# Attention into two expert layers: row sums from a column of ones, and one transpose for two heads

## The chip, the core and the metric

One core of a Trainium2 chip runs the whole program. Its engines run side by side, each through its own queue in order: PE multiplies matrices (PEld is its weight load), DVE, ACT and POOL work element by element, and SP issues the transfers (DMA). An engine that waits for another holds everything behind the waiting instruction. The metric is the device time of one execution in microseconds; less is better.

## What is computed

```python
B, H, S, D = 4, 8, 576, 64
scores = np.matmul(q, k.transpose(0, 1, 3, 2)) / sqrt(D)
x = (log1p(abs(rel)) / psi_i)[..., None]          # rel[i, j] = i - j
bias = np.maximum(x @ w1 + b1, 0.0) @ w2          # 32 hidden, one bias per head
scores = scores + bias.transpose(2, 0, 1)[None]
attn = exp(scores - max(scores)); attn = attn / (sum(attn) + 1e-09)
x = np.matmul(attn, v)          # -> 2304 tokens x 512
r = np.maximum(x @ w_in, 0.0); x = (s * r * r + b) @ w_out       # 512 -> 2048 -> 512
h = x @ w_in2; out = (h - np.tanh(h)) @ w_out2                   # 512 -> 2048 -> 512
```

In the text the first layer after attention is MoE1 and the second MoE2.

## The kernel before

Every float32 operand of a product is split into two float16 parts, hi and lo, and a product is made of several float16 products (hi x hi, hi x lo, lo x hi). DVE, ACT and POOL do the splitting: a cast gives hi, and a subtraction gives lo.

**Bias.** For each of 36 blocks Q of 16 rows, `hid` (L717, instructions at L727 on ACT and L730 on DVE or POOL) makes the 32 hidden values for up to 576 distances in tiles `hid`, `hr` or `xt_own` (whichever memory is free then), PE multiplies them into `pb` (L761), `out` (L766, through `copy_scale`, L611 on DVE, L615 on ACT) writes the row and its mirror image into a tile `et`, and SP sends it to a buffer `btd` in memory, from which `bi` is read row by row.

**Attention.** 36 groups of four units; a unit is one head on 128 rows of queries (or two heads on 64). For a unit, `qk` (L1030) multiplies queries and keys into `sp` (two units in one go), `ttr` (L1073, DVE) adds the bias and takes the minimum of the negated scores, `mx_add` (L1081) adds a constant to it, `ex` (L1087, ACT) takes the exponential `e` and, by a read of ACT's accumulator, its row sum, `hi` (L1097 DVE, L1099 ACT) and `lo` (L1104) split `e` into `hl`, `tr` (L1119) turns `hl` over by a DMA transpose of nine 128x128 blocks (five of hi, four of lo, the fifth being shared) into `et`, and `pv` (L1132 for v's hi part, L1138 for its lo part) multiplies `et` with the values `vp` into the PSUM tile `xp`, of which there is one buffer for the four units of a group. When a group is done, `x_tasks` adds a small constant to the sums (`eps`, L1176), takes reciprocals (L1180), scales `xp` (L1188), splits the result and turns it over by transposes of four blocks (L1217) for MoE1.

**MoE1** starts while attention runs. For a block of 256 tokens, `ph` (L1573) is the first product, `relu` (L1586) and `square` (L1591) follow on ACT, the result is split into `hr` (`hi` L1597 DVE or L1599 ACT, `lo` L1603), and `po` (L1645) is the second product, whose output leaves PSUM at L1659 (DVE) or L1664 (ACT) as `x`. `norm` (L1554) stands before the first `ph`. **MoE2** starts when attention's memory is free: its weights are converted and prepared there (`w2big`, `w1big`; L618 writes a low part), and then seven block products in place of eight run through `pa`, `pb` (L2038) and `acc` (L2166).

**The order.** Nothing is issued in the order of the program text. `Schedule` holds all tasks with the engines that each may use, an estimated duration for each, what it depends on, which tiles it takes from a ring of buffers and a priority. `forward` plays them through with a clock for each engine, takes the task that can start first, with priorities to decide between tasks that can start at almost the same time, and so writes out each engine's queue. The tables `COST` and `XFER` multiply the estimates of operations and transfers, `ENGINE` limits a task to an engine, `SHIFT` adds to priorities, and `PORT` says which DVE tasks the planner keeps from running beside POOL's. The rings hold two `e`, three `hl`, four `et` and four `bi`; `ENGINE` and these tables name tasks by stage and function (`u3.hi`: cast of the exponentials in the third stretch of units).

## Time and profile before

| | |
|---|---|
| time, median of 3 runs | 1053.97 us (1053.57 to 1055.98) |
| the profiled execution | 1057.96 us |
| its span in the trace | 1056.2 us |
| granted clock of PE over the span, mean | 0.954 |
| busy: PE, DVE, ACT, POOL | 964.1 (91%), 881.6 (83%), 667.5 (63%), 250.1 us (24%) |
| instructions on PE, DVE, ACT, POOL | 13486, 1918, 1307, 319 |
| row sums (L1087, accumulator reads) | 144, 28.1 us on ACT |
| DMA transposes of exponentials (L1119) | 144, from 66.6 to 566.1 us |

The span is the time from the first to the last instruction in the trace, and the time of an execution has a little around it. An engine's share of busy time is an average over stretches with different limits, so that it must be read by stretch. A group of instructions is a line of the program on one engine, with the tiles written and read; "x28 | 13.8, 498" says that 28 instructions took 13.8 us in all, 498 ns each in the mean. What stands behind the second bar is the engine's idle time just before them, with what ended it.

### The profile page before, as it was taken

How to read it: one execution, taken by the hardware profiler on the slowest of the kernel's cores; microseconds unless marked ns; L12 is line 12 of the kernel's file. 1: busy time of each engine (PE TensorE's matmuls, PEld its weight loads, DVE VectorE, ACT ScalarE, POOL GpSimd, SP SyncE). 2: the span in 40 equal slices, each digit the busy share in tenths (PEclk: the TensorE clock that was granted, in tenths of full speed). 3: DMA queues.
4: the chain of work that ended last, by engine and by line, in shares of the span. 5: the costliest groups of instructions: out<-in, count | busy, mean ns of one | idle time of the engine just before them, and what ended most of it. 6: DMA issues, size and time to landing. Idle time of an engine off the chain costs nothing.

```text
span 1056.2 us, 32450 instructions
## 1 busy us (share of the span) xinstructions
PE 964.1 (91%) x13486; PEld 833.2 (79%) x13486; DVE 881.6 (83%) x1918; ACT 667.5 (63%) x1307; POOL 250.1 (24%) x319
## 2 busy tenths in 40 slices
...
GB/s 341 398 227 216 311 236 119 184 200 252 245 197 230 168 179 176 201 188 207 171 180 104 397 21 138 148 36 12 32 23 32 52 23 22 42 22 23 22 22 22
DMA packets 261444, 153.66 MB, mean 145 GB/s; under 512 B 197680, under 2 KB 229552, under 8 KB 261296
## 3 DMA queue, kind: packets, MB, share of 16 engines
...
## 4 chain that ended last, share of the span: by engine, by line
PE 43%; DVE 9%; ACT 3%; DMA 2%; issue 2%; POOL 1%; SPq 0%; DVEq 0%; ACTq 0%; POOLq 0%
PE acc L2166 14%; PE pa L2038 9%; PE pb L2038 7%; PE po L1645 5%; PE ph L1573 4%; PE po L2166 2%; DMA et<-hl 2%; DVE w2big L1852 2%; DVE w2big L618 1%; PE sp L1041 1%; DVE w1big L618 1%; ACT e L1087 1%; POOL hl L1104 1%; PE xp L1132 1%; DVE hr L1603 1%
## 5 line engine op out<-in xcount | busy, mean ns | idle before, releaser
L1645 PE MATMUL po<-hr,w1big 128*128 128x256 f16 x1728 | 202.9, 274 | 3.6 <-ACT x L1664 2.7
L1104 POOL TENSOR_TENSOR hl<-e,hl 128x64 f16<-128x64 f32 (+1 forms) x200 | 160.2, 818 | 184.9 <-ACT hl L1099 107.2
L1573 PEld LDWEIGHTS <-w1big 128*128 128x128 f16 x1728 | 166.9, 99 | 31.5 <-issue 10.6
L1645 PEld LDWEIGHTS <-w1big 128*128 128x128 f16 x1728 | 165.5, 98 | 26.5 <-issue 7.1
L2038 PEld LDWEIGHTS <-w2big 128*128 128x128 f16 x3024 | 175.2, 99 | 2.2 <-issue 2.1
L2166 PEld LDWEIGHTS <-w1big 128*128 128x128 f16 x3024 | 172.8, 98 | 0.0
L1087 ACT ACTIVATE e<-sp,mx 128x576 f32<-128x576 f32 x144 | 105.6, 735 | 70.3 <-POOL mx L1081 34.3
L1073 DVE CUSTOM_DVE_ANT_0 sp<-sp,bi 128x576 f32<-128x576 f32 x144 | 107.0, 772 | 20.2 <-PE sp L1041 16.2
L1573 PE MATMUL ph<-xt_own,w1big 128*128 128x256 f16 x960 | 113.1, 274 | 3.0 <-ACT r L1586 2.2
L1041 PE MATMUL sp<-ks,qs 64*128 64x288 f16 (+1 forms) x960 | 84.2, 296 | 25.8 <-ACT e L1087 24.8
L1573 PE MATMUL ph<-w1big 128*128 128x256 f16 x768 | 91.2, 276 | 3.3 <-ACT r L1586 2.6
L1041 PEld LDWEIGHTS <-qs 64*128 64x128 f16 (+1 forms) x960 | 48.7, 99 | 53.0 <-issue 42.2
L1132 PEld LDWEIGHTS <-et 128*128 128x128 f16 (+1 forms) x1440 | 54.7, 104 | 41.2 <-issue 21.5
L1132 PE MATMUL xp<-vp,et 128*128 128x64 f16 (+1 forms) x1440 | 65.4, 199 | 19.1 <-DMA et<-hl 11.7
L2166 PE MATMUL acc<-hr,w1big 128*128 128x128 f16 x1296 | 79.9, 219 | 0.0
L1099 ACT ACTIVATE hl<-e 128x576 f16<-128x576 f32 x96 | 64.7, 678 | 23.1 <-DMA et<-hl 20.2
L2166 PE MATMUL acc<-w2big,w1big 128*128 128x128 f16 x1296 | 79.0, 219 | 0.0
L1104 DVE TENSOR_TENSOR hl<-e,hl 128x512 f16<-128x512 f32 (+1 forms) x88 | 48.8, 572 | 15.9 <-ACT hl L1099 13.0
L2038 PE MATMUL pa<-w1big,w2big 128*128 128x128 f16 x960 | 59.9, 219 | 1.7 <-ACT w2big L2057 0.9
L1586 ACT ACTIVATE r<-ph 128x512 f32<-128x512 f32 x72 | 42.3, 590 | 25.8 <-PE ph L1573 21.3
L1591 ACT ACTIVATE r<-r,sq 128x512 f32<-128x512 f32 x72 | 51.2, 718 | 0.9
L2074 ACT ACTIVATE w1big<-w1big 128x512 f32<-128x512 f32 x34 | 21.3, 630 | 45.6 <-DVE w1big L2064 33.4
...
## 6 DMA issues: line engine op xcount, KB each, us to landing
...
```

Of the source, the lines that this page charges most:

```text
L1041: nc.tensor.matmul(out=out, lhsT=qs.tile[64 * h:64 * h + 64, sq, p * r:p * r + r], rhs=ks.tile[64 * h:64 * h + 64, sk, half * HS:(half + 1 ...
L1073: nc.vector.tensor_tensor_reduce(out=st, in0=st, in1=bi.tile.rearrange("p (a b) -> p a b", a=2), scale=-1.0 / KAP, scalar=3.0e38, op0=ALU. ...
L1087: nc.scalar.activation(out=put(e, row_tile("e")).rearrange("p (a b) -> p a b", a=2), in_=sp.tile[:, :, 0:HS], func=AF.Exp, scale=-1.0, bia ...
L1099: nc.scalar.activation(out=h[:, 0:S], in_=e.tile, func=AF.Copy)
L1104: eng_of(eng).tensor_tensor(out=hl.tile[:, o:o + m], in0=e.tile[:, c:c + m], in1=hl.tile[:, c:c + m], op=ALU.subtract)
L1132: nc.tensor.matmul(out=xp[r0:r0 + r, o:o + 64], lhsT=et.tile[:, n, r0:r0 + r], rhs=vp.tile[:, 0, n % 5, 64 * h:64 * h + 64], start=n == 0, ...
L1573: nc.tensor.matmul(out=ph.tile[:, fi, :], lhsT=win_ap(1, sw, m, f), rhs=xa(sx, m), start=m == 0 and j == 0, stop=m == KM - 1 and j == 2,)
L1586: nc.scalar.activation(out=r.tile, in_=ph.tile, func=AF.Relu)
L1591: nc.scalar.activation(out=r.tile, in_=r.tile, func=AF.Square, scale=sq[:, fp // 4:fp // 4 + 1])
L1645: nc.tensor.matmul(out=po.tile[:, :NB1], lhsT=wout_ap(1, sw, f, c), rhs=rhl[f // 8][:, f % 8, sr, :], start=f == 0 and j == 0, stop=f == K ...
L2038: nc.tensor.matmul(out=bank.tile[:, f * HT:(f + 1) * HT], lhsT=w[:, sw, m, f * 128:(f + 1) * 128], rhs=xs[:, sx, m], start=p in (1, 2, 5) ...
L2166: nc.tensor.matmul(out=bank.tile[:, o + c * HT:o + (c + 1) * HT], lhsT=w[:, sw, f, c * 128:(c + 1) * 128], rhs=g[:, sx, f], start=new and ...
```

## The change

The changed kernel makes the row sums of the softmax on PE. The hi part of `vp` gets a 65th column of ones for each head (a memset, `ones`), nine of the 14 `pv` matmuls of a unit write 65 columns, and `xp` has 260 columns in place of 256. The exponential no longer reads the accumulator, and the order that the sums imposed on the exponentials of a group is gone; `eps` reads the sums out of `xp` when all four `pv` of the group are done, on DVE alone.

The exponentials of two units share one tile `hl` and one tile `et` of twice the size. One DMA transpose of 18 blocks takes the place of two of nine, and the `pv` of both units come after it. The rings hold two of each, where they held three `hl` and four `et`. Two blocks Q of the bias share an `et` tile as well.

More tasks may choose their engine: `mx_add` may go to ACT (50 of 144 do), `hid` of every block Q to POOL (`QG` from 7 to 36), `relu` to DVE (11 of 72 do), and the copies of the first products out of PSUM to DVE (17 do, at L2057 in the kernel before). The matrix of ones on the diagonal that `norm_max` multiplies with is bfloat16. The planner's estimates, its hops between engines and the tables are new; of the tables one or two lines stand here.

```diff
-SHARE0, QP, QA, SCU, QG = 21, 8, 16, 12, 7
+SHARE0, QP, QA, SCU, QG = 21, 8, 16, 12, 36
...
-AHEAD = 6.97
+AHEAD = 8.21
...
-    "x.recip": 0.0,
+    "x.recip": 0.0, "x.eps": 0.0,
...
-    "s1.lambda": "dve", "f1.hi": "act", "bias3.out": "act", "bias4.lambda": "dve", "k1.hi": "act", "f2.hi":
+    "s1.lambda": "dve", "f1.hi": "act", "bias3.out": "act", "bias4.lambda": "act+dve", "f2.hi": "dve",
...
-    HOP = dict(pe=0.57, act=-0.03, dve=0.16, pool=0.37, turn=0.0)
+    HOP = dict(pe=0.57, act=-0.05, dve=0.12, pool=0.41, turn=0.0)
...
-                    elif eng == "pool" and t.opts[eng] < self.LONG:
+                    elif eng == "pool" and t.share > 0.0 and t.opts[eng] < self.LONG:
...
-    ROWS = dict(bi=4, e=2, hl=3, et=4)
+    ROWS = dict(bi=4, e=2, hl=2, et=2)
...
-    xp_all = ps_x.tile([128, 256], F32, name="xp")
+    xp_all = ps_x.tile([128, 260], F32, name="xp")
...
-        t = row_p.tile([128, S + 16 if name == "et" else S], F32, tag=name, name=name, bufs=ROWS[name])
-        return t if dt == F32 else t[:, :S].bitcast(dt)
+        n = {"et": 2 * S + 32, "hl": 2 * S}.get(name, S)
+        t = row_p.tile([128, n], F32, tag=name, name=name, bufs=ROWS[name])
+        return t if dt == F32 else t[:, :min(n, 2 * S)].bitcast(dt)
...
-    eye32 = const.tile([128, 128], F32, name="eye32")
+    eye16 = const.tile([128, 128], BF16, name="eye16")
...
             if Q < QG:
-                opts[POOL] = 4.2e-3 * n
+                opts[POOL] = 5.0e-3 * n
...
-        ev = inst("et")
+        ev = ev_of[Q] = ev_of[Q - 1] if Q % 2 else inst("et")
+        eo = Q % 2 * (S + 16)
...
-            o = put(ev, row_tile("et"))
+            o = (ev.tile if Q % 2 else put(ev, row_tile("et")))[:, eo:]
...
-        t_ev = [sc.add({ACT: 0.87, DVE: 0.80}, out, t_bmm[Q], d, [ev], [i])]
+        t_ev = [sc.add(
+            {ACT: 0.87, DVE: 0.80}, out, t_bmm[Q] + (t_evs[Q - 1] if Q % 2 else []), d, [] if Q % 2 else [ev], [i, ev]
+        )]
+        t_evs[Q] = t_ev
...
-            t = put(vp, vp_p.tile([128, 2, VW], F16, tag="vp", name="vp").rearrange("p s (n c) -> p s n c", c=128))
-            copy_scale(t[:, 0], src(), sc_t[b]["v"], eng)
+            t = vp_p.tile([128, 2 * VW + 10], F16, tag="vp", name="vp")
+            put(vp, (
+                t[:, :VW + 10].rearrange("p (n h d) -> p n h d", h=2, d=65),
+                t[:, VW + 10:].rearrange("p (n h d) -> p n h d", h=2, d=64),
+            ))
+            copy_scale(vp.tile[0][:, :, :, 0:64], src().rearrange("p n (h d) -> p n h d", h=2), sc_t[b]["v"], eng)
...
+        def ones(eng):
+            eng_of(eng).memset(vp.tile[0][:, :, :, 64:65], 1.0)
+        to = sc.add({POOL: 0.15, DVE: 0.1}, ones, [th], due - 2, [], [vp], share=0.0)
...
-        vp, sm_i, xp_i = vp_t[b, p], sum_of[n], xp_of[n]
+        e = inst("e")
+        odd = k % 2
+        hl, et = hl_of[u], et_of[u] = (hl_of[u - 1], et_of[u - 1]) if odd else (inst("hl"), inst("et"))
+        h0 = odd * 2 * S
+        vp, xp_i = vp_t[b, p], xp_of[n]
         mx = {}
...
-        t_mx = sc.add({DVE: 0.16, POOL: 0.3}, mx_add, [t_ttr[u]], d + 1.5)
+            if eng == ACT:
+                nc.scalar.activation(out=m, in_=m, func=AF.Copy, bias=LN_E)
+            else:
+                eng_of(eng).tensor_scalar(out=m, in0=m, scalar1=LN_E, scalar2=None, op0=ALU.add)
+        t_mx = sc.add({DVE: 0.16, POOL: 0.31, ACT: 0.2}, mx_add, [t_ttr[u]], d + 1.5)
 
...
-            if k == 0:
-                put(sm_i, sm.tile([128, NP], F32, tag="sum", name="sum"))
             nc.scalar.activation(
                 out=put(e, row_tile("e")).rearrange("p (a b) -> p a b", a=2), in_=sp.tile[:, :, 0:HS], func=AF.Exp,
-                scale=-1.0, bias=mx["m"][:, 0:1], accum_out=sm_i.tile[:, col:col + 1],
-            )
-        t_exp[u] = sc.add({ACT: 0.78}, ex, [t_mx], d + 2, [e] + ([sm_i] if k == 0 else []), [sp, sm_i],
-                           [t_exp[u - 1]] if k else [])
+                scale=-1.0, bias=mx["m"][:, 0:1],
+            )
+        t_exp[u] = sc.add({ACT: 0.695}, ex, [t_mx], d + 2, [e], [sp])
...
-            h = put(hl, row_tile("hl", F16))
+            h = (hl.tile if odd else put(hl, row_tile("hl", F16)))[:, h0:h0 + S]
...
+        if not odd:
+            return
+
         def tr(_):
             nc.sync.dma_start_transpose(
                 out=put(et, row_tile("et", F16).rearrange("p (n r) -> p n r", r=128)), in_=hl.tile
             )
-        t_tr[u] = sc.add({SP: (1.25, 1.4)}, tr, t_lo, d + 5 - 500, [et], [hl])
+        t_tr[u] = t_tr[u - 1] = sc.add({SP: (1.4, 2.8)}, tr, t_los[u - 1] + t_lo, d + 5 - 500, [et], [hl])
+        for v in (u - 1, u):
+            unit_pv(v)
+
+    def unit_pv(u):
...
-            o = col * 64
+            o = col * 65
...
-                        out=xp[r0:r0 + r, o:o + 64], lhsT=et.tile[:, n, r0:r0 + r],
-                        rhs=vp.tile[:, 0, n % 5, 64 * h:64 * h + 64], start=n == 0, stop=False,
+                        out=xp[r0:r0 + r, o:o + 65], lhsT=et.tile[:, e0 + n, r0:r0 + r],
+                        rhs=vp.tile[0][:, n % 5, h], start=n == 0, stop=False,
...
-            {PE: 0.42 if full else 0.85}, pv, [t_tr[u], t_vlo[b, p], t_pv.get(u - 1)], d + 10 - 1000,
+            {PE: 0.42 if full else 0.85}, pv, [t_tr[u], t_pv.get(u - 1)] + t_vlo[b, p], tau(u) + 10 - 1000,
...
-        def eps(eng):
-            ri = sum_of[n].tile
-            eng_of(eng).tensor_scalar(out=ri, in0=ri, scalar1=1e-9 * 2.0 ** 15, scalar2=None, op0=ALU.add)
-        te = sc.add({DVE: 0.16, POOL: 0.3}, eps, [t_exp[u] for u in us], d - 3, [], [sum_of[n]])
+        sums = inst("sum")
+        x65 = lambda: xp_of[n].tile.rearrange("p (h d) -> p h d", d=65)
+
+        def eps(_):
+            t = put(sums, sm.tile([128, NP], F32, tag="sum", name="sum"))
+            nc.vector.tensor_scalar(
+                out=t, in0=x65()[:, :, 64], scalar1=1e-9 * 2.0 ** 15, scalar2=None, op0=ALU.add
+            )
+        te = sc.add({DVE: 0.18}, eps, [t_pv[u] for u in us], d - 502, [sums], [xp_of[n]], share=0.0)
 
         def recip(_):
-            nc.vector.reciprocal(out=sum_of[n].tile, in_=sum_of[n].tile)
-        te = sc.add({DVE: 0.17}, recip, [te], d - 2, [], [sum_of[n]])
+            nc.vector.reciprocal(out=sums.tile, in_=sums.tile)
+        te = sc.add({DVE: 0.17}, recip, [te], d - 501, [], [sums])
 
         xf = inst("xf")
 
         def scale(_):
-            x = xp_of[n].tile.rearrange("p (h d) -> p h d", d=64)
+            x = x65()[:, :, 0:64]
             put(xf, x_p.tile([128, 256], F32, tag="xf", name="xf", bufs=2))
             nc.vector.tensor_tensor(
                 out=xf.tile.rearrange("p (h d) -> p h d", d=64), in0=x,
-                in1=sum_of[n].tile.unsqueeze(2).to_broadcast([128, NP, 64]), op=ALU.mult,
-            )
-        t_xs[n] = sc.add({DVE: 0.41}, scale, [t_pv[u] for u in us] + [te], d - 500, [xf], [sum_of[n], xp_of[n]], share=0.0)
+                in1=sums.tile.unsqueeze(2).to_broadcast([128, NP, 64]), op=ALU.mult,
+            )
+        t_xs[n] = sc.add({DVE: 0.41}, scale, [te], d - 500, [xf], [sums, xp_of[n]], share=0.0)
...
-            nc.tensor.matmul(out=pm.tile, lhsT=m.to_broadcast([128, 128]), rhs=eye32, start=True, stop=True)
+            nc.tensor.matmul(out=pm.tile, lhsT=m.to_broadcast([128, 128]), rhs=eye16, start=True, stop=True)
...
+                if e == DVE:
+                    nc.vector.tensor_scalar(out=r.tile, in0=ph.tile, scalar1=0.0, scalar2=None, op0=ALU.max)
+                else:
+                    nc.scalar.activation(out=r.tile, in_=ph.tile, func=AF.Relu)
...
-                {ACT: 0.68}, lambda _: nc.scalar.activation(out=home(i), in_=bank.tile, func=AF.Copy, scale=ich),
-                [t] + (first_use["E"] if k < 2 else []), pr - 300, [i], [bank],
+                {ACT: 0.68, DVE: 0.66}, lambda e: copy_scale(home(i), bank.tile, ich, e),
+                [t] + (first_use["E"] if k < 2 else []), pr - 300, [i], [bank], share=0.0,
```

Because the planner writes the queues, the order of the work moves too, in three places above all.

On DVE, at the start of the program, `u_sb` is the table of logarithms from which the hidden layer is made in `hr`; `gram`, `qk_t`, `qk_y` and `qkc` belong to the scan that gives the scales of queries and keys. Before:

```order
L701 TENSOR_SCALAR u_sb<-w1big,cst_sb 128x576
L730 TENSOR_SCALAR hr<-u_sb,cst_sb 128x576 x2
L730 TENSOR_SCALAR hr<-u_sb,cst_sb 128x560 x2
L730 TENSOR_SCALAR hr<-u_sb,cst_sb 128x544 x2
L896 TENSOR_REDUCE s_0_127<-gram 128x2
L730 TENSOR_SCALAR hr<-u_sb,cst_sb 128x528 x2
L815 TENSOR_SCALAR qk_t<-psum 128x2
L807 TENSOR_SCALAR qk_y<-qk_t 128x2
```

And in the changed kernel, the same place:

```order
L706 TENSOR_SCALAR u_sb<-w1big,cst_sb 128x576
L907 TENSOR_REDUCE s_0_127<-gram 128x2
L826 TENSOR_SCALAR qk_t<-psum 128x2
L818 TENSOR_SCALAR qk_y<-qk_t 128x2
L823 TENSOR_SCALAR qk_t<-qk_y 128x1
L829 SCALAR_TENSOR_TENSOR qk_t<-qk_t,qk_y 128x1
```

The hidden layer has left this place of DVE's queue; ACT and POOL do it.

On SP, where the transposes of the first units meet the bias rows that are written to memory (`btd<-et`) and read back (`bi<-btd`) and the loads of MoE1's weights (`w1big<-in_wout`). Before:

```order
L468 DMA w1big<-in_wout 128x2x1024
L468 DMA bi<-btd_119 128x576 x2
L1119 DMA_TRANSPOSE et<-hl 128x9x128 x3
L468 DMA bi<-btd_119 128x576 x2
L468 DMA btd_121<-et 128x591 x2
L1119 DMA_TRANSPOSE et<-hl 128x9x128
L1217 DMA_TRANSPOSE xt_own<-xh 128x4x128
L1119 DMA_TRANSPOSE et<-hl 128x9x128 x2
```

And in the changed kernel:

```order
L472 DMA w1big<-in_wout 128x2x1024
L1149 DMA_TRANSPOSE et<-hl 128x18x128
L472 DMA btd_120<-et 128x591 x2
L472 DMA bi<-btd_119 128x576 x2
L1149 DMA_TRANSPOSE et<-hl 128x18x128
L472 DMA btd_121<-et 128x591 x2
L1149 DMA_TRANSPOSE et<-hl 128x18x128
```

One issue stands where two stood, and it stands where the second of a pair stood or later: no `pv` of a pair can begin before it.

On PE, at the end of MoE1, each matmul has a weight load before it in the queue. Before, the first product of MoE2 (`pa`, with weights `w2big`) comes straight behind 144 `po`, and only products follow:

```order
L1645 LDWEIGHTS w1big
L1645 MATMUL po<-hr,w1big 128x256
L2038 LDWEIGHTS w2big
L2038 MATMUL pa<-w1big,w2big 128x128
L2038 LDWEIGHTS w2big
```

In the changed kernel 96 `po` stand before the first `pa`, and 48 more come after 24 matmuls each of `pa` and `pb`; this is the place where `pb` ends and those 48 begin:

```order
L2089 LDWEIGHTS w2big
L2089 MATMUL pb_11412<-w1big,w2big 128x128
L1696 LDWEIGHTS w1big
L1696 MATMUL po<-hr,w1big 128x256
L1696 LDWEIGHTS w1big
```

Up to the last `pv`, PE's queue holds 1104 `po` and 1248 `ph` before the change, 1056 and 1248 after it.

## Rows read from the trace of the kernel before

**Rows 1.** Windows: stretch and length us, busy us (count) PE PEld DVE ACT POOL, clock, DMA, GB/s

```profile
20.00:160.00 140.00, 92.70 (x891) 51.07 (x892) 133.66 (x266) 104.69 (x216) 61.35 (x55) 0.73 0.96 281
...
200.00:560.00 360.00, 348.06 (x4641) 289.25 (x4637) 261.43 (x719) 246.24 (x557) 154.96 (x236) 1.00 0.99 198
560.00:620.00 60.00, 54.71 (x574) 47.62 (x573) 39.06 (x78) 29.78 (x72) 1.64 (x3) 0.97 0.65 213
620.00:703.00 83.00, 77.72 (x705) 68.69 (x704) 80.64 (x124) 64.63 (x115) 0.00 (x0) 1.00 0.32 101
703.00:724.00 21.00, 15.34 (x230) 14.79 (x228) 20.20 (x26) 15.35 (x21) 0.00 (x0) 0.90 0.03 9
724.00:1056.00 332.00, 328.19 (x5845) 328.02 (x5843) 300.33 (x605) 163.31 (x246) 0.00 (x0) 0.99 0.09 28
```

**Rows 2.** Waits: engine, line, releaser: us in all, times, longest (PE from 150 us)

```profile
PE sp L1041 <- ACT e L1087: 8.8, 14, 2.3
PE xp L1132 <- DMA et<-hl: 5.6, 6, 2.5
...
ACT hl L1099 <- DMA et<-hl: 20.2, 22, 2.5
```

**Rows 3.** Groups of DVE: line, form, count, busy us, mean ns, idle before

```profile
L618 DVE SCALAR_TENSOR_TENSOR w2big<-w2big,w_c 128x1024 f16<-128x1024 f32 x14 | 17.6, 1280 | 0.4 <-ACT w2big L615 0.4
...
L1659 DVE TENSOR_SCALAR x<-po,esc,bcol 128x128 f32<-128x128 f32 (+1 forms) x41 | 14.4, 395 | 19.7 <-PE po L1645 19.7
L730 DVE TENSOR_SCALAR hid<-u_sb,cst_sb 128x400 f32<-128x400 f32 (+8 forms) x27 | 14.0, 556 | 2.1 <-PE pb L761 2.0
L1597 DVE CAST hr<-r 128x512 f16<-128x512 f32 x28 | 13.8, 498 | 7.7 <-ACT r L1591 7.6
...
L730 DVE TENSOR_SCALAR hr<-u_sb,cst_sb 128x576 f32<-128x576 f32 (+6 forms) x12 | 6.6, 593 | 3.8 <-PE pb L761 3.8
...
L611 DVE TENSOR_SCALAR et<-pb,cst_sb 128x496 f32<-128x496 f32 (+11 forms) x12 | 5.7, 519 | 0.3 <-PE pb L761 0.3
```

**Rows 4.** Groups of ACT, and one of POOL

```profile
L1087 ACT ACTIVATION_READ_ACCUMULATOR e<-sp,mx 128x1 f32 x144 | 28.1, 195 | 0.0
L615 ACT ACTIVATE et<-pb,cst_sb 128x576 f32<-128x576 f32 (+59 forms) x60 | 26.9, 500 | 17.5 <-PE pb L761 16.7 <-DMA btd<-et 0.7
...
L727 ACT ACTIVATE hr<-u_sb,cst_sb 128x416 f32<-128x416 f32 (+14 forms) x36 | 20.9, 644 | 1.2 <-DVE u_sb L701 1.2
...
L730 POOL TENSOR_SCALAR hr<-u_sb,cst_sb 128x512 f32<-128x512 f32 (+5 forms) x8 | 20.8, 2608 | 9.4 <-PE pb L761 5.2 <-DVE u_sb L701 4.0 <-DVE qkc L824 0.2
```

**Rows 5.** Tile et: transposes on SP, ns min/median/max of the issue; time to landing

```profile
L1119 SPq DMA_TRANSPOSE et<-hl x144: 1241/1350/4232, 66.6 to 566.1; - x144
...
DMA to landing us min/median/max: 2.1/4.0/12.0
```

**Rows 6.** Line L1217, transposes of four blocks: the same

```profile
L1217 SPq DMA_TRANSPOSE xt_own<-xh x16: 1189/1220/2143, 92.6 to 556.7; - x16
...
DMA to landing us min/median/max: 2.5/3.8/5.6
```

**Rows 7.** Groups of DVE: reciprocal and eps of the sums

```profile
L1180 DVE RECIPROCAL sum<-sum 128x4 f32<-128x4 f32 x36 | 6.2, 172 | 0.5
...
L1176 DVE TENSOR_SCALAR sum<-sum 128x4 f32<-128x4 f32 x29 | 5.5, 189 | 11.9 <-ACT e L1087 11.7
```

**Rows 8.** Timeline of PE: start us, duration us, line, form, count

```profile
571.12 0.47 PE L1132 MATMUL xp<-vp,et 128*64 128x64 f16 x18
...
698.39 5.40 PE L1645 MATMUL po<-hr,w1big 128*128 128x256 f16 x48 [1.60 <-ACT x L1664]
703.63 1.50 PE L2038 MATMUL pa<-w1big,w2big 128*128 128x128 f16 x24
```

**Rows 9.** Groups of DVE by form, from 580 to 700 us, then 200 to 560

```profile
L1603 DVE TENSOR_TENSOR hr<-r,hr 128x512 f16<-128x512 f32 x22 | 14.8, 688 | 1.1 <-ACT hr L1599 1.0
...
L1603 DVE TENSOR_TENSOR hr<-r,hr 128x512 f16<-128x512 f32 x30 | 23.6, 792 | 2.5 <-ACT hr L1599 2.2
```

119 lines of the change are left out of this document (66 added, 53 removed), and 269 rows, old and new, of tables (ENGINE, SHIFT).

## The prediction

> **What bounds the kernel now.** I read the busy times by stage first [rows 1], then what PE waits for [rows 2], then the groups of instructions of the stages that are not PE's [rows 3, 4], then the transposes [rows 5, 6] and the seam between the two halves [rows 8]. The reader should see three regimes in [rows 1].
>
> From 20 to 160 us DVE is busy 133.66 of 140 us and PE only 92.70, at a granted clock of 0.73 (a mix of the two levels, 1.2 and 2.4 GHz, since PE stands idle again and again there). This is the start: bias, scans, weight conversion and the first attention units. DVE's queue sets its pace; ACT is at 104.69 of 140.
>
> From 200 to 560 PE is busy 348.06 of 360 at a full clock: the rest of attention runs between MoE1's matmuls, and only 11.9 us of PE is idle. DVE (261) and ACT (246) have room. What is saved on them here is worth nothing unless it removes one of PE's own waits; the largest of those after 150 us are 8.8 us for the exponentials and 5.6 us for transposed blocks [rows 2].
>
> After the last attention matmul, at 571 us [rows 8], comes a seam. PE has MoE1's remaining matmuls (1104 by the order; 48 take 698.39 to 703.63, 5.24 us [rows 8], so 120.5 us), and MoE2's first product starts at 703.63. From 620 to 703 DVE is busy 80.64 of 83 us with the weights of MoE2, so that DVE sets the start of the products; then PE loses another 5.7 us up to 724 (15.34 of 21 busy). From 724 on PE is busy 328 of 332 us. That last third has the same products in both kernels and cannot shrink.
>
> So the time is: length of the start, plus PE's work and waits, plus the seam.
>
> **The start.** Up to the first block's norm (L1554) the new DVE queue lacks twelve hidden-layer instructions in hr (12 x 0.593 = 7.1 us), eight of ten that write bias rows into et (8 x 0.519 = 4.2) and six hidden-layer ones in hid (6 x 0.556 = 3.3) [rows 3]: 14.6 us; the rest of the stretch balances. They go to ACT and POOL. ACT has, up to its first relu, eight more for hr and its spare buffer and four more for hid (12 x 0.644 = 7.7) and eight more for et (8 x 0.500 = 4.0), and loses 24 accumulator reads of the exponentials (24 x 0.195 = 4.7) [rows 4]: +7.0 us. POOL does 12 hidden-layer instructions there instead of 8, +4 x 2.608 = 10.4 us [rows 4]. If DVE alone counted, the start would be 14.6 us shorter. ACT then has 104.7 + 7.0 us to do in 140 - 14.6 us, 89%, in a chain in which ACT and DVE wait for each other, and POOL's 12 instructions (12 x 2.608 = 31 us one behind the other) stand ahead of the first bias rows. I take half, **-7 us**, with 0 and -14.6 as ends.
>
> **Exponentials and sums.** The accumulator read goes from all 144 exponentials (28.1 us of ACT [rows 4]); after 200 us ACT is covered by PE, so nothing. The sums now come out of PE: nine of 14 matmuls of a unit have 65 columns for 64. No row shows 65; by the 256-column matmuls' pace in [rows 8] (5.24 us for 48, so 0.43 ns a column) it is 144 x 9 x 0.43 ns = 0.6 us. In return the sum's eps and reciprocal (0.189 and 0.172 us [rows 7]) now stand between the last pv matmul of a group and its scaling, and xp has one buffer, so the next group's first pv waits 0.4 us longer. In the old order the next pv followed at once or within 2 us of PE work at 9 of 35 group borders (counted from the order, each matmul at its row's pace); in the new order there are at least 1.3 us of other matmuls at each, 4.7 us at the median, so this is hidden. Without that cover it would be 36 x 0.4 = 14 us.
>
> **Transposes.** 72 of 18 blocks instead of 144 of 9. The issue on SP took 1.22 us (median) with 4 blocks and 1.35 with 9 [rows 5, 6]; on that line 18 blocks take some 1.6 us, and SP gets 144 x 1.35 - 72 x 1.6 = 79 us back. SP is not the bound, so this counts for nothing by itself, though bias and q loads behind a transpose go out sooner. Landing took 3.8 us (median) with 4 blocks [rows 6] and 4.0 with 9, with 2.1 and 12.0 as extremes [rows 5]; on that line 18 take 4.4, though the DMA engines are at 0.99 from 200 to 560 [rows 1] and the same blocks have to pass through them. The two halves of a pair went out one behind the other on the same queue before; if the blocks take their time, the second half lands no later than now, and only the first is held back. Between a pair's qk and its pv the old order has 11.1 (first) and 13.0 us (second) of PE work at the median of units 88 to 135, the new one 14.2 and 14.6: 3 us more for the first, 1.6 for the second. I take **0**, with -5 (the transposes' waits in [rows 2] gone) and +12 as ends: no row shows 18 blocks.
>
> **PE's order.** 48 MoE1 matmuls (po) move from before attention's last pv to after it, 5.2 us by [rows 8]; hence the last pv comes that much earlier, and with it everything that waits for attention's memory, MoE2's weights above all. The count between last pv and first product is the same in both orders; the 48 now stand behind the first products, where PE lost 5.7 us. **-5 us**, 0 if that gap stays and they come on top.
>
> **The seam.** From the last scaling to the second low part of the first x block (the last thing that the first product needs) DVE now has seven more casts of hr (7 x 0.498) and six more output copies (6 x 0.395) and two weight instructions less (2 x 1.280) [rows 3]: 3.5 + 2.4 - 2.6 = +3.3 us. Part lies before 620 us, where DVE has 39 of 60 us. **+2**, from -1.6 to +4. Past it DVE has some 12 us of weight preparation left over that it used to have done, and 17 copies out of PSUM taken over from ACT; DVE was at 300 of 332 us there [rows 1], so I take 0, up to +6.
>
> **PE's waits from 200 to 560.** They total 11.9 us; 21 low parts of hr (0.75 us each, between 0.688 and 0.792 [rows 9]) went from DVE to POOL, 15.7 us. **-2**, from -8 to +6.
>
> **Sum.** -7 + 0 - 5 + 2 - 2 = -12 us. The profiled execution took 1057.96 us, of which the span is 1056.20; it lies 0.4% above the median of 1053.97. I take the 12 us from the median: **1042 us**.
>
> **Rivals.**
> - *Slower: PE waits for the 18-block transposes.* PE is in order, and pv stands at a fixed place in its queue. Against: 1.6 to 3 us more work stand in front of pv. For: hl and et now have two buffers of two units, so a late landing also holds back the next pair's casts (ACT waited 20.2 us for that already, 22 times [rows 2]). Each 1 us by which a pair is late costs up to 72 us; from 0.17 us a pair (12 / 72) the gain is gone. With 0.4 us, 29 us: about 1071.
> - *The start is not shortened.* ACT, or POOL's chain of bias rows, takes DVE's place. ACT at 89% speaks for it, the 140 us of slack-free DVE against it. The 7 us go: 1049.
> - *POOL holds DVE up.* The low parts of hr on DVE took 0.688 us when POOL was silent and 0.792 while it worked [rows 9]. If POOL's extra 10.4 us are taken from DVE one for one, the start keeps 4.2 of 14.6, half of that by the reasoning above, 2 for 7: about 1047. The Trainium skill (SBUF — State Buffer, section SBUF: two separate sides) has such a rule: the port pair of GpSimd and VectorE is locked for a whole instruction, and the loser is fully blocked. Rows 9 show 0.1 us per instruction, much less than a full block at each meeting; by the full lock the sum would be this rival's.
> - *The order gains more.* The start by 14, waits by 8: 1030.
> - *Off the path.* Start and 48 matmuls come back as waits of PE later: 1053.
>
> **How the numbers follow.** Forecast (1035 to 1048) 0.38; more 0.15; start not shortened 0.14; POOL 0.05; off the path 0.13; slower 0.15. A change below 0.3% (3.2 us) can't be told from none here. The first four are faster by more: 0.72; same 0.13; slower 0.15. The range leaves out most of the slower case and the far end of the better one: 1029 to 1057.
>
> **What would show it.** DVE's busy share of the start falls and the first block's norm comes some 7 us earlier; last pv near 557 (571 less 14); first product near 692; PE full behind it, where 5.7 us are lost now; the same 332 us of products. Waits of PE for et<-hl stay under 12 us in all. It is wrong if they grow to tens of us, if the start's DVE share falls below 90% without the norm moving, or if PE shows gaps after 724.

## The result

The changed kernel takes 1064.26 us (median of 4 runs, 1060.99 to 1066.43) against 1053.96 of the kernel before: a ratio of 1.0085, with an interval of 1.0058 to 1.0112. A gain of 12 us was forecast, and a loss of 10 came by the medians (9 by the ratio, 6 to 12 by its interval), outside the range of 1029 to 1057. Single executions of one kernel lie several us apart (the kernel before took 1050 to 1061 in the 21 runs beside e1), and most of what differs lies ahead of attention's last pv: in two traces of the changed kernel it ended at 575.0 and 570.5 us, and from there to the end it was 489.6 and 489.7. So a difference of 2 or 3 us between two traces says little ahead of that point. Behind it the products are the firm stretch (see below); the seam and the products together still vary by 3 us, from 481.2 to 484.2 in eight traces of kernels that do the same work there as the kernel before.

The same stretches as in [rows 1], of the kernel after (columns as there; this execution took 1066.43 us, its span is 1064.6):

```profile
20.00:160.00 140.00, 85.87 (x799) 44.15 (x797) 126.90 (x233) 106.61 (x204) 73.70 (x61) 0.79 0.94 275
200.00:560.00 360.00, 339.75 (x4436) 280.08 (x4428) 257.15 (x684) 245.73 (x501) 163.96 (x206) 0.99 0.94 196
560.00:620.00 60.00, 53.39 (x672) 45.80 (x670) 39.74 (x71) 30.75 (x71) 1.80 (x3) 1.00 0.74 227
620.00:703.00 83.00, 80.31 (x734) 71.80 (x735) 79.28 (x150) 57.54 (x103) 0.00 (x0) 1.00 0.29 96
703.00:724.00 21.00, 17.34 (x227) 15.95 (x225) 20.14 (x33) 14.21 (x20) 0.00 (x0) 1.00 0.13 38
724.00:1056.00 332.00, 328.83 (x5845) 328.56 (x5845) 312.94 (x612) 161.58 (x241) 0.00 (x0) 0.99 0.09 26
```

DVE is 6.8 us less busy in the start than in [rows 1] (126.90 for 133.66), not 14.6, and nothing came of it: the first norm (L1599 now) begins at 147.5 us, after 146.3. In attention PE is idle for 20.3 of 360 us instead of 11.9, although ACT and DVE have no more to do. Cut at the events rather than at fixed times, the comparison is clearer. First the kernel before, then the kernel after, from the start to the first norm, to the end of the last pv, to the first product, to the end:

```profile
0.00:146.30 146.30, 90.92 (x849) 48.26 (x850) 130.72 (x257) 104.42 (x211) 63.93 (x56) 0.76 0.94 294
146.30:572.00 425.70, 406.01 (x5462) 332.99 (x5459) 314.94 (x844) 291.84 (x651) 185.49 (x262) 0.98 0.96 191
572.00:703.60 131.60, 124.27 (x1114) 109.66 (x1114) 116.04 (x190) 92.59 (x179) 0.67 (x1) 0.99 0.43 151
703.60:1056.20 352.60, 342.93 (x6066) 342.26 (x6064) 319.93 (x629) 178.66 (x266) 0.00 (x0) 0.99 0.09 27
```

```profile
0.00:147.50 147.50, 87.60 (x842) 45.71 (x842) 121.66 (x227) 110.79 (x210) 78.99 (x66) 0.82 0.94 290
147.50:575.00 427.50, 402.69 (x5421) 326.83 (x5419) 313.92 (x811) 296.34 (x595) 198.96 (x241) 0.98 0.93 190
575.00:706.30 131.30, 122.49 (x1114) 108.62 (x1112) 114.35 (x201) 85.02 (x162) 0.00 (x0) 1.00 0.42 150
706.30:1064.60 358.30, 347.16 (x6114) 345.66 (x6112) 332.69 (x649) 172.74 (x257) 0.00 (x0) 1.00 0.09 27
```

The start is 1.2 us longer, attention 1.8 us longer with 48 matmuls less in it (PE's busy time falls by 3.3), the seam the same, and the products are 5.7 us longer: 358.3 for 352.6. This last difference is the firm one. In eleven further traces of the old order of `po` and products the last stretch took 351.3 to 352.9 us, in six of the new order 358.0 to 358.5; the means lie 6.4 us apart. The trace of the kernel before is of an execution 4 us above that kernel's median, the other 2 us above its own, so that these two traces show a little less than the whole loss.

In the products PE's timeline shows where the 48 matmuls went (columns as in [rows 8]; in brackets the idle time before a row and what ended it):

```profile
706.33 1.50 PE L2089 MATMUL pa<-w1big,w2big 128*128 128x128 f16 x24
707.67 1.50 PE L2089 MATMUL pb<-w1big,w2big 128*128 128x128 f16 x24
709.01 5.40 PE L1696 MATMUL po<-hr,w1big 128*128 128x256 f16 x48
715.42 0.38 PE L700 MATMUL psum<-cols,ones 128*128 128x2 f32 x2 [1.00 <-DVE cols L1947]
...
719.29 1.50 PE L2089 MATMUL pb<-w1big,w2big 128*128 128x128 f16 x24 [0.79 <-ACT w2big L620]
720.63 1.50 PE L2089 MATMUL pa<-w1big,w2big 128*128 128x128 f16 x24
726.16 4.47 PE L2089 MATMUL pa<-w1big,w2big 128*128 128x128 f16 x48 [4.03 <-ACT w1big L620]
```

The 48 `po` at 709.01 lie between the products as the order said, but PE's waits there are not gone: 4.03 us of waiting for `w1big` are still there, behind them, as 3.87 us were in the kernel before at this place (with the smaller ones 5.8 us in all, for 5.6 before):

```profile
720.47 0.56 PE L695 MATMUL psum<-cols,ones 128*128 128x2 f32 x2 [3.87 <-DVE w2big L2064]
```

What PE waits for there is the end of a chain on DVE and ACT. DVE has more to do behind the seam than before, 332.69 us for 319.93. What the 48 did for the waits is read from e8, which takes them away from here.

The change did move what it says. The groups of DVE, ACT and POOL that answer to [rows 3, 4, 7]:

```profile
L735 DVE TENSOR_SCALAR hid<-u_sb,cst_sb 128x496 f32<-128x496 f32 (+8 forms) x18 | 9.9, 558 | 0.0
...
L1219 DVE TENSOR_SCALAR sum<-xp 128x4 f32<-128x4 f32 x36 | 5.6, 155 | 7.2 <-PE xp L1178 7.0
...
L616 DVE TENSOR_SCALAR et<-pb,cst_sb 128x272 f32<-128x272 f32 (+3 forms) x4 | 1.9, 516 | 0.3 <-PE pb L769 0.3
...
L620 ACT ACTIVATE et<-pb,cst_sb 128x576 f32<-128x576 f32 (+33 forms) x68 | 30.4, 502 | 7.3 <-PE pb L769 4.5 <-DMA btd<-et 2.0 <-PE xp L1178 0.5
L732 ACT ACTIVATE hr<-u_sb,cst_sb 128x448 f32<-128x448 f32 (+15 forms) x46 | 27.6, 673 | 1.1 <-DVE u_sb L706 1.1
...
L735 POOL TENSOR_SCALAR hr<-u_sb,cst_sb 128x512 f32<-128x512 f32 (+7 forms) x10 | 24.3, 2438 | 13.0 <-PE pb L769 9.1 <-DVE u_sb L706 4.0
```

No hidden layer in `hr` is left on DVE, ACT has 46 of them for 36 and 68 copies into `et` for 60, and the accumulator reads are gone.

The waits of PE from 150 us, and ACT's wait for a free `hl`, which answer [rows 2]:

```profile
PE sp L1061 <- ACT e L1112: 8.8, 9, 1.5
PE xp L1172 <- DMA et<-hl: 5.6, 9, 2.0
...
ACT hl L1123 <- DMA et<-hl: 11.1, 10, 2.8
```

From 150 us PE's waits for blocks and for exponentials are no longer than before, 5.6 and 8.8 us. Over the whole program they are longer for the blocks; the first of these rows is of the kernel before, the second of the kernel after:

```profile
PE xp L1132 <- DMA et<-hl: 11.7, 11, 2.5
...
PE xp L1172 <- DMA et<-hl: 19.6, 14, 4.1
```

So all of the growth lies in the first 150 us (14.1 us there, 6.1 before), a stretch that [rows 2] leaves out.

The transposes, which answer [rows 5]:

```profile
L1149 SPq DMA_TRANSPOSE et<-hl x72: 2400/3366/8317, 68.5 to 568.8; - x72
...
DMA to landing us min/median/max: 2.1/5.3/12.8
```

The issue of 18 blocks holds SP for 3.37 us, not the 1.6 of the prediction's line, and the blocks land after 5.3 us, not 4.4.

### The profile page after: what moved, and what is told of

The parts are those of the page before. It is cut to its first block, busy times and chain, and to the rows that moved or that the text cites. A ratio compares the mean times of both kernels' runs of the same rounds, so it can differ in the third digit from the quotient of the medians.

```text
span 1064.6 us, 32073 instructions
## 1 busy us (share of the span) xinstructions
PE 959.9 (90%) x13484; PEld 826.8 (78%) x13484; DVE 882.6 (83%) x1885; ACT 664.9 (62%) x1224; POOL 277.9 (26%) x307
## 4 chain that ended last, share of the span: by engine, by line
PE 45%; DVE 18%; DMA 9%; ACT 2%; issue 2%; SPq 1%; POOL 0%; DVEq 0%; ACTq 0%; POOLq 0%
PE ph L1618 10%; PE acc L2217 10%; PE po L1696 8%; PE pa L2089 6%; DMA et<-hl 5%; PE pb L2089 4%; PE sp L1061 2%; DVE w1big L623 2%; PE xp L1172 2%; DVE w2big L623 2%; PE po L2217 2%; DVE w2big L2143 1%; DVE hr L623 1%; DVE w2big L1301 1%; DVE w2big L1903 1%
## 5 line engine op out<-in xcount | busy, mean ns | idle before, releaser
L1130 POOL TENSOR_TENSOR hl<-e,hl 128x64 f16<-128x64 f32 (+1 forms) x165 | 152.3, 937 | 144.6 <-ACT hl L1123 91.9
L1061 PE MATMUL sp<-ks,qs 64*128 64x288 f16 (+1 forms) x960 | 80.4, 293 | 23.2 <-ACT e L1112 19.6
L1061 PEld LDWEIGHTS <-qs 64*128 64x128 f16 (+1 forms) x960 | 46.0, 98 | 50.0 <-issue 36.6
L1172 PE MATMUL xp<-vp,et 128*128 128x65 f16 (+1 forms) x1440 | 66.0, 199 | 19.9 <-DMA et<-hl 19.6
L1130 DVE TENSOR_TENSOR hl<-e,hl 128x64 f16<-128x64 f32 (+1 forms) x123 | 64.2, 536 | 16.5 <-ACT hl L1123 14.8
L1123 ACT ACTIVATE hl<-e 128x576 f16<-128x576 f32 x89 | 58.7, 677 | 11.5 <-DMA et<-hl 11.1
L1654 POOL TENSOR_TENSOR hr<-r,hr 128x512 f16<-128x512 f32 x37 | 46.3, 1253 | 34.2 <-ACT hr L1650 25.4
```

What stands on the lines that cost most here:

```text
L1061: nc.tensor.matmul(out=out, lhsT=qs.tile[64 * h:64 * h + 64, sq, p * r:p * r + r], rhs=ks.tile[64 * h:64 * h + 64, sk, half * HS:(half + 1 ...
L1123: nc.scalar.activation(out=h, in_=e.tile, func=AF.Copy)
L1130: eng_of(eng).tensor_tensor(out=hl.tile[:, h0 + o:h0 + o + m], in0=e.tile[:, c:c + m], in1=hl.tile[:, h0 + c:h0 + c + m], op=ALU.subtract,)
L1172: nc.tensor.matmul(out=xp[r0:r0 + r, o:o + 65], lhsT=et.tile[:, e0 + n, r0:r0 + r], rhs=vp.tile[0][:, n % 5, h], start=n == 0, stop=False,)
```

## Experiments

Each ratio is that of the run to runs of the kernel before on the same chip, with its 95% interval. The edits change what a task issues or where it stands; the planner's order is otherwise kept, so that a kernel differs from its base in the lines that are named and in no others. The diffs are shortened, and a name like `po_behind` or `low_parts_are_issued` stands for a search that the run's kernel writes out. A number from a single trace has the uncertainty named above: in traces of kernels whose start is that of the kernel before, the first norm came between 145.6 and 147.1 us.

**e1, two transposes of nine for one of 18, at the same place.**

```diff
-            nc.sync.dma_start_transpose(out=put(et, ...), in_=hl.tile)
+            o = put(et, ...)
+            for h in range(2):
+                nc.sync.dma_start_transpose(out=o[:, 9 * h:9 * h + 9], in_=hl.tile[:, 2 * S * h:2 * S * h + 2 * S])
```

> The changed kernel, where each DMA transpose of 18 blocks is issued as two of nine, one right behind the other at the same place in SP's queue; every other queue is word for word the same. The changed kernel took 1064.3 us, the kernel before 1054.0. Theory A (the size of one transfer costs: an 18-block issue held SP for 3.37 us where two of nine would hold it for 2.7, and PE's waits for transposed blocks grew from 11.7 to 19.6 us): the first half lands 1 to 2 us sooner, PE's waits for et<-hl fall to about 12 us, and the time to 1057 to 1060. Theory B (the pairing costs, that both halves are issued only when the second unit's low parts are done): the time stays within 1062 to 1066. Theory C (neither; the new order of the queues has lost elsewhere): as B.

Measured: 1.0072 (1.0044 to 1.0101).

**e5, the changed kernel again**, as measure for e1 and those that follow.

> The changed kernel itself, beside the other runs of this chip, as their measure. It took 1.0085 (1.0058 to 1.0112) of the kernel before. Both theories: 1.006 to 1.010 of the kernel before. If it is clearly above the 1.0072 of the run with two transposes of nine blocks, the size of the transposes has a price after all; if equal, it has none that can be measured.

Measured: 1.0093 (1.0061 to 1.0125). The transposes of e1:

```profile
L1151 SPq DMA_TRANSPOSE et<-hl x144: 1253/1356/6266, 67.1 to 565.1; - x144
...
DMA to landing us min/median/max: 2.1/4.0/12.9
```

Issue and landing are back at the 1.36 and 4.0 us of [rows 5], and the time is that of the changed kernel within what can be told (the intervals overlap by far). The size of a transpose is not what makes the loss; 2 us by the two ratios may hang on it, which is within the error. PE's waits for blocks did shrink, from 19.6 us to 9.3.

**e2, the first half of a pair as soon as it is ready.**

```diff
+        def early():
+            if not odd and low_parts_are_issued(u) and has_free_buffer(et):
+                put(et, ...)
+                nc.sync.dma_start_transpose(out=et.tile[:, 0:9], in_=hl.tile[:, 0:2 * S])
```

> The changed kernel with two transposes of nine blocks for one of 18, of which the first is issued as soon as its own unit's low parts are done and a buffer of et is free (69 of 72 pairs move it ahead in SP's queue); PE, DVE, ACT and POOL keep the order of the changed kernel. Theory A (size): like the run with two transposes at one place, 1057 to 1060. Theory B (pairing): PE's waits for et<-hl fall from 19.6 us (with 27.5 more at the weight loads) to about the 11.7 (and 18.1) of the kernel before, and the time falls by 5 to 8 us, to 1056 to 1059, clearly below the run with both at one place. Theory C (the order has lost elsewhere): 1062 to 1066.

Measured: 1.0149 (1.0109 to 1.0189), worse than the pair at one place, so that holding the first half back is not what costs. The rest of the pairing is still in this kernel: `hl` and `et` with two buffers of two units each, and both `pv` behind the second unit. Why it is worse was not found: PE's waits for blocks are as short as in e1 (8.1 us, 9.3 there), those for exponentials longer (22.4 us, 16.9 there):

```profile
PE sp L1082 <- ACT e L1133: 22.4, 22, 2.4
...
PE xp L1208 <- DMA et<-hl: 8.1, 5, 4.3
```

**e3, the ones column alone, in the kernel before.**

```diff
-                ... bias=mx["m"][:, 0:1], accum_out=sm_i.tile[:, col:col + 1],
+                ... bias=mx["m"][:, 0:1],
...
+            nc.gpsimd.memset(vp.tile[0][:, :, :, 64:65], 1.0)
...
-                        out=xp[r0:r0 + r, o:o + 64], ... rhs=vp.tile[:, 0, n % 5, 64 * h:64 * h + 64]
+                        out=xp[r0:r0 + r, o:o + 65], ... rhs=vp.tile[0][:, n % 5, h]
```

> The kernel before with the row sums alone changed: a column of ones beside the values, 65 columns in nine of 14 pv matmuls, no accumulator read behind the exponentials; eps and reciprocal stand right before the scaling of the group on DVE. The order of all queues is otherwise that of the kernel before. The prediction's steps (28.1 us of ACT gone under PE's cover, 0.6 us of columns, 0.4 us between a group's last pv and its scaling): within 1050 to 1055. Rival (the sums on the path of xp cost: each of 36 groups holds the next group's pv by 0.4 us, 14 us in all where no other work covers it): 1060 to 1068.

Measured: 1.0021 (0.9999 to 1.0043). The 28.1 us of ACT bring nothing. A small cost is not excluded and not shown. PE's waits for the scaling are 8.4 us (six times) for 5.2 (twice) before, as the rival would have it, but e11, which has no column of ones, shows 8.4 us as well:

```profile
PE xp L1136 <- DVE xf L1195: 8.4, 6, 2.6
```

**e12, both edits to the computation undone in the changed kernel** (sums from the accumulator as before, and the transposes of e1), so that the new order is left with its engines, and with the pairing of units in `hl`, `et` and `pv`.

```diff
+                ... bias=mx["m"][:, 0:1], accum_out=acc_of[n][:, col:col + 1],
...
-                        out=xp[r0:r0 + r, o:o + 65], ... rhs=vp.tile[0][:, n % 5, h]
+                        out=xp[r0:r0 + r, o:o + 64], ... rhs=vp.tile[0][:, n % 5, h, 0:64]
...
-                out=t, in0=x65()[:, :, 64], scalar1=1e-9 * 2.0 ** 15
+                out=t, in0=acc_of[n], scalar1=1e-9 * 2.0 ** 15
```

> The changed kernel with both of its edits to the computation undone: the sums come from the accumulator of ACT again (64 columns in pv; eps and reciprocal stay where they are), and each transpose of 18 blocks goes out as two of nine at one place. What is left is the new order with its choice of engines, and the pairing. Theory O (the order and the engines in it cost): 1.006 to 1.011 of the kernel before, as the changed kernel (1.0093). Theory E (the edits cost; alone the ones column gave 1.0021, two transposes for one 1.0072): 0.999 to 1.004.

Measured: 1.0085 (1.0064 to 1.0105), the ratio of the changed kernel itself. The loss lies in what is left, not in the ones column or in the size of the transposes. Between the order, its engines and the pairing this run does not decide.

**e4, DVE's early work to ACT, in the kernel before.**

```diff
+        if eng == DVE and not norm_seen:      # hid, and the same in out
+            eng = ACT
```

> The kernel before with every hidden-layer instruction and every bias copy that DVE does ahead of the first block's norm given to ACT, at the same places in the order (20 instructions or so leave DVE); all else as before. Theory of the prediction (DVE sets the pace of the start, 14.6 us of it leave): the first norm comes 5 to 10 us earlier than 146.3, the time is 1044 to 1049. Rival (DVE's work there stood in the shadow of loads and of PE, ACT and the bias chain): the first norm moves by less than 2 us, or later since ACT has 15 us more, and the time is 1053 to 1062; DVE's idle time ahead of the scan (s<-gram) grows to some 8 us, as in the changed kernel.

Measured: 1.0039 (1.0016 to 1.0061); the first norm comes at 148.8 us, 2.5 later. DVE's waits in the start, of the kernel before, of e4 and of the changed kernel:

```profile
DVE s L896 <- PE gram L868: 1.5, 1, 1.5
...
DVE s L902 <- PE gram L874: 7.5, 1, 7.5
...
DVE s L907 <- PE gram L879: 7.8, 1, 7.8
```

The freed DVE stands 7.5 us for the first scan, whose keys are not there sooner, and 7.8 us in the changed kernel. What the scan waits for in its turn showed in the kernel before:

```profile
PE gram L868 <- DMA w1big<-in_kT: 11.9, 3, 7.5
```

**e7, the twelve instructions in `hr` left out of DVE, and given to nobody.**

```diff
-        if eng == ACT:
+        if eng == DVE and not norm_seen and Q < QA:
+            del hid_t[Q, t]                   # the product reads another tile of the block
+        elif eng == ACT:
```

> The kernel before without the hidden-layer instructions that DVE writes into hr ahead of the first norm (12, 7.1 us; the product reads another of the block's hidden tiles in their place, so the bias is not the reference's); nothing is given to another engine. Theory of the prediction (DVE sets the pace of the start): the first norm comes 4 to 7 us earlier than 146.3, the time is 1047 to 1050. Rival 1 (other engines: the twelve filled DVE's waits for keys and scans): the norm moves by less than 2 us and the time by less than 3. With ACT loaded instead (the run that gave all to ACT) the norm came 2.5 us later; if here it comes 4 to 7 us earlier, ACT had taken DVE's place; if it does not move, DVE was never the bound there.

Measured: 0.9972 (0.9953 to 0.9991), 3 us; the first norm at 144.4, 1.9 earlier. Even as a gift 7.1 us of DVE are worth some 3, and where ACT has to take them over, with the bias rows, as in e4, less than nothing.

**e17 and e18, exactly the change's engines for the hidden layer and bias copies of the first 24 blocks:** taken out of the changed kernel, and put into the kernel before.

```diff
+    early_eng = {"hid0.0": "act", "hid0.1": "pool", ... "out5.0": "act", ...}     # e18; e17 the reverse
...
+        eng = early_eng.get(f"hid{Q}.{t}", eng)
```

> The changed kernel, where the hidden layer and the bias copies of the first 24 blocks run on the engines that the kernel before gives them (12 hidden-layer instructions and four bias copies back on DVE, 8 in place of 12 on POOL, the rest on ACT); all queues are otherwise in the order of the changed kernel. Theory S (the start's choice of engines is part of the loss, as giving DVE's early work to ACT cost 1.0039 in the kernel before): 1.004 to 1.007 of the kernel before, for 1.0093 without. Rival (the engines of the start are worth nothing either way, the loss is in the rest of the order): 1.008 to 1.011.

> The mirror: the kernel before, where the hidden layer and the bias copies of the first 24 blocks run on the engines that the changed kernel gives them (DVE is rid of 12 and of four copies, POOL has 12 in place of 8, ACT the rest). Theory of the prediction (DVE sets the pace of the start): first norm 5 to 9 us earlier, 0.990 to 0.996. Theory S: first norm within 2 us or later, 1.002 to 1.005. Rival: 0.999 to 1.002.

Measured: e18 1.0036 (1.0013 to 1.0059), with the first norm at 151.7 us; e17 1.0111 (1.0086 to 1.0136). Put into the kernel before, the choice costs 4 us where 7 were forecast as gain. Taken out of the changed kernel, it gives nothing back. That the order around it was made for these engines would explain this, and is not shown. So what the start adds to the loss can't be read off by undoing it.

**e6, 188 matmuls of po left out in the middle of attention, in the kernel before.**

```diff
+                            if n == 3 and (f or j):
+                                continue
```

> The kernel before, where the second product of MoE1 for the fourth block of 256 tokens leaves out 188 of its 192 matmuls (one of each column block is left, so the result of these tokens is not the reference's); they lie in the middle of attention. At 5.24 us for 48 they are 20.5 us of PE. Theory P (PE bounds attention, as the prediction said): last pv and the end come 15 to 21 us earlier, 1034 to 1040. Theory F (these matmuls only fill PE's time between the steps of attention, whose pace another chain sets): last pv moves by 0 to 6 us, time 1048 to 1054, and PE's idle time between the first norm and the last pv grows from 19.7 to 33 us or more. Under F, moving 48 of them behind attention can't have brought its 5 us.

Measured: 0.9992 (0.9970 to 1.0014). PE has 20.5 us less to do, and the time does not change. From the first norm to the last pv, then the stretch in which most of these matmuls are missing, and the same stretch of the kernel before:

```profile
147.10:570.90 423.80, 395.67 (x5275) 320.45 (x5271) 312.78 (x844) 292.04 (x651) 186.50 (x262) 0.95 0.95 192
...
400.00:450.00 50.00, 42.94 (x517) 33.16 (x516) 35.47 (x102) 34.69 (x77) 22.84 (x36) 0.78 1.04 188
...
400.00:450.00 50.00, 48.26 (x644) 40.28 (x639) 35.49 (x100) 33.64 (x77) 22.75 (x37) 1.00 1.10 198
```

Last pv is over at 570.9, after 572.0. Of the 20.5 us, some 8 went into idle time (28.1 us for 19.7) and some 10 into a lower granted clock, since PE's busy time fell by 10.3 us only (395.67 for 406.01): from 400 to 450 PE had 517 matmuls for 644, was busy for less of the stretch, and the clock, a mix of 1.2 and 2.4 GHz, fell to 0.78, so that the fewer matmuls took 42.94 us for 48.26. The lower clock takes part of the test away. What is left of it is that PE is 10.3 us less busy and attention ends 1.1 us sooner, which is within what single traces differ by.

**e10, transposes of five blocks for nine from the 41st unit on, in the kernel before** (the low parts' blocks are left out, and `pv` reads the hi blocks in their place).

```diff
+            m = 9 if u < 40 else 5
-                out=put(et, ...), in_=hl.tile
+                out=put(et, ...)[:, :m], in_=hl.tile[:, :m * 128]
```

> The kernel before, where from the 41st unit on a transpose turns five blocks (the hi part) in place of nine, and pv reads the hi blocks in place of the four lo ones (so the low part of the weights is wrong); 104 of 144 transposes carry 4/9 less, all other work is the same. Theory D (the DMA engines, at a busy share of 0.99 from 200 to 560 us, set the pace of attention): last pv comes more than 10 us earlier and the time is under 1045. Theory C (the chain of engines from scores to exponentials sets it): last pv moves by less than 4 us, time 1050 to 1057.

Measured: 0.9900 (0.9869 to 0.9931), 10.5 us. From the first norm to the last pv (columns as above, the last two the DMA engines' busy share and GB/s):

```profile
146.30:559.20 412.90, 401.99 (x5462) 331.36 (x5459) 314.93 (x844) 291.28 (x651) 186.59 (x262) 0.99 0.79 164
```

Attention takes 412.9 us for 425.7, with the same work on PE, DVE, ACT and POOL and a DMA share of 0.79 for 0.96. Transfers have a hand in attention's pace, 12.8 us here; taking load off PE (e6) moved it by 1.1. Whether it is the DMA engines' load or the earlier landing of the blocks is not told apart.

**e11, without mx_add, in the kernel before.**

```diff
-            eng_of(eng).tensor_scalar(out=m, in0=m, scalar1=LN_E, scalar2=None, op0=ALU.add)
+            pass
```

> The kernel before without the small instruction between the minimum and the exponential (mx_add, 144 of 128x1 on DVE or POOL), which leaves out a constant factor of exponentials and sums. Theory C (a chain in which qk waits for a free sp, sp for the exponential, and that for the minimum, sets attention's pace): one hop of 0.3 to 0.6 us goes from each step of it, ACT's waits for mx (53.7 us, 39 times) and PE's for e (24.8 us) shrink, and last pv comes 8 to 25 us earlier; time 1030 to 1047. Theory D (DMA): last pv moves by less than 4 us, time 1050 to 1056.

Measured: 0.9964 (0.9947 to 0.9982), 3.5 us: between the two theories. A hop less helps, but 0.3 us a unit, the least that was put down for the hop, would have been 43 us if each were on the path. Of the kernels here that compute everything but this factor it is the fastest, and it beats both. (The factor makes the exponentials larger in float16; whether a kernel should do without it is a question of accuracy that times don't answer.)

**e9, the last 48 po moved from ahead of the last pv to right behind it, in the kernel before** (four tasks of 12; the outputs of these `po` on DVE and ACT and their stores move with them).

```diff
+        move = set(po_ahead_of_last_pv[-4:])
+        seq = [t for t in seq[:last + 1] if t not in move] + moved + seq[last + 1:]
```

> The kernel before with the last 48 po matmuls ahead of attention's last pv moved right behind it (their output and its store move with them; nothing else). This is the prediction's step by itself. Theory of the prediction (PE bounds attention): last pv comes 5 us earlier than 571.6, near 566, and what follows with it, so that the time is 1049 to 1054. Theory F (these matmuls only fill waits of PE): last pv stays within 2 us of 571.6, the 48 come on top behind it, and the time is 1057 to 1060.

Measured: 1.0073 (1.0048 to 1.0098), 6.4 us. From the first norm to the last pv, to the first product, to the end:

```profile
145.60:569.20 423.60, 402.89 (x5416) 330.02 (x5413) 313.48 (x841) 291.61 (x651) 185.66 (x262) 0.98 0.95 192
569.20:706.70 137.50, 129.73 (x1162) 114.49 (x1161) 116.98 (x192) 92.47 (x179) 0.67 (x1) 0.99 0.41 145
706.70:1059.60 352.90, 343.18 (x6066) 342.51 (x6064) 319.77 (x629) 178.60 (x266) 0.00 (x0) 0.99 0.09 27
```

The step that the prediction put at -5 us, done alone, is a loss. The seam grows by 5.9 us (137.5 for 131.6), a little more than the matmuls moved into it; attention, rid of them, gives back 2.8 at most.

**e8, the 48 po of the changed kernel back in front of the first product.**

```diff
+        move = po_behind(first_product) + what_they_need_of(seq[first_product:])
+        seq = seq[:first_product] + move + [t for t in seq[first_product:] if t not in move]
```

> The changed kernel with the 48 po matmuls that stand behind the first products put back in front of them, as in the kernel before (what they need on DVE and ACT moves with them, nothing else does). Theory Z (they cost 5.2 us wherever they stand, and the change only carried them from one stretch into another): the first product comes about 5 us later than in the changed kernel, near 711, the stretch after it is 353 instead of 358 us, and the time is that of the changed kernel within 2 us. Theory of the prediction (behind the first products they fill a gap of 5.7 us): the time grows by 3 to 5 us. Theory G (they hold the weights' chain up where they stand now): the time falls by 3 to 5 us.

Measured: 1.0103 (1.0069 to 1.0137), within the interval of e5. From the last pv to the first product, and to the end:

```profile
576.40:714.30 137.90, 127.79 (x1161) 113.24 (x1160) 120.77 (x205) 88.38 (x167) 0.00 (x0) 1.00 0.40 145
714.30:1069.40 355.10, 342.71 (x6066) 341.96 (x6064) 326.39 (x643) 169.79 (x252) 0.00 (x0) 0.99 0.09 26
```

The seam is 6.5 us longer (137.9 for 131.4), the products only 3.2 shorter (355.1 for 358.3). So by this trace the 48 cost 3 us less between the products than ahead of them: without them PE's waits there are 7.8 us (2.81 and 4.98) in place of 5.8. They did fill some 2 us, as the prediction meant, but of a gap that is longer in the new order. With the same 6066 matmuls as in the kernel before, the products still take 355.1 us for 352.6, with 326.39 us of work on DVE for 319.93. The ratio, with its wide interval, can neither confirm nor deny these 3 us.

**e13 and e14, 48 po more ahead of the last pv,** in the kernel before and in the changed one, with their outputs on DVE and ACT.

```diff
+        for i in range(A0, n_in + 4):
+            j = i - 4 * (i - A0 + 1) / (n_in + 4 - A0)
+            place(po[i], max(old_place(j), behind_what_it_needs(po[i])))
```

> The kernel before with 48 more po matmuls ahead of the last pv (1152 in place of 1104): from the 57th group of 12 on each stands a little earlier in PE's queue, as far as what it needs allows, and the outputs of po with them on DVE and ACT. It is the mirror of the run that moved 48 behind (1.0073). Theory F (attention's pace is not PE's, matmuls in it are free, behind it they cost 5.2 us for 48): 0.993 to 0.997 of the kernel before, with the time from last pv to the end 5 us shorter. Theory P (PE bounds attention): last pv 5 us later, 0.999 to 1.003.

> The changed kernel with the same: 48 more po ahead of the last pv, so that there are 1104 of them as in the kernel before. Theory F: 1.003 to 1.006 of the kernel before, for 1.0093 without. Theory P: 1.008 to 1.011. If it falls below 1.003, the move of po was all of the loss.

Measured: e13 1.0039 (1.0017 to 1.0060), e14 1.0228 (1.0197 to 1.0260). The seam of e13, and e14 from its first norm to the last pv:

```profile
574.40:705.00 130.60, 120.45 (x1066) 105.64 (x1066) 116.20 (x190) 92.42 (x179) 0.67 (x1) 0.97 0.43 152
...
146.60:589.40 442.80, 409.30 (x5467) 331.60 (x5465) 313.22 (x811) 295.16 (x595) 195.48 (x241) 0.98 0.88 184
```

So matmuls in attention are not free either: in e13 last pv ends 2.4 us later (574.4), and the rest of the program is only 1.1 us shorter (483.1 for 484.2); the times, 4 us longer by the ratio, agree that more was lost ahead of the last pv than won behind it. Theory F holds for matmuls that are taken out, not for ones that are put in. A likely reason is that one put ahead of a pv or qk in PE's queue delays what is behind it. It is not enough for e14, where 48 matmuls, some 5 us, make attention 15 us longer (442.8 for 427.5); why was not found. For the changed kernel this means that putting the 48 back does not undo its loss.

**e15, the moves of e4 and e9 together in the kernel before; e16, those of e11 and e13.**

> The kernel before with two single runs put together: the early work of DVE on the hidden layer and the bias rows given to ACT (1.0039 alone) and the last 48 po moved behind the last pv (1.0073 alone). If the two moves of the new order are causes that stand side by side: 1.009 to 1.013, which is the changed kernel's loss (1.0085 with both edits to the computation undone). If they overlap: 1.006 to 1.009.

> The kernel before with 48 more po ahead of the last pv and without mx_add (a constant factor of exponentials and sums is left out; alone it gave 0.9964). Theory F, both gains side by side: 0.990 to 0.994. If po in attention is not free: 0.995 to 0.999.

Measured: e15 1.0067 (1.0036 to 1.0098), no more than e9 alone: as far as the intervals tell, the two losses do not add up. e16 1.0027 (1.0010 to 1.0044): the gain of e11 is used up by the loss of e13, and no kernel better than e11 came of it.

## Why the prediction was wrong

**The start, -7 us: wrong; 1.2 us were lost in the traces.** A busy share of 95% was read as a bound. The twelve instructions stood in DVE's queue where it would have waited for the scan of keys; without them it waits (7.8 us in the changed kernel, 7.5 in e4, 1.5 before). The test of that reading was in reach: PE's waits of the kernel before hold 11.9 us for the keys that the scan needs. And work given to ACT (in e18 also to POOL) costs: e4 and e18 took 4 us more each. That ACT, at 75% of the start, sits in a chain in which an instruction more is a delay would explain it, and is argued. The rival that the start is not shortened had the mechanism, but ended at no gain where a loss was to be had.

**PE's order, -5 us: wrong, and the largest part of the loss that can be shown.** The step held two claims. One was that attention ends 5.2 us sooner with 48 matmuls less, since PE is busy for 97% of it; its other end, 0, took this gain for granted too. e6 takes out four times as many, PE is 10.3 us less busy, and attention ends 1.1 us sooner; e9 takes out the 48 and gains 2.8 at most. The other was that they fill PE's gap at the first products. By e8 they fill some 2 us, but PE's waits there, 5.8 us, are as long as before, and the stretch is 5.7 us longer. A move from a stretch where PE is not the bound to one where it is costs its price at the new place. By e9 the move alone, to the place right behind the last pv, is 1.0073; by the events of the traces the products hold 5.7 of the changed kernel's 8.4 us.

**DVE behind the first product, 0: too small.** The prediction saw that DVE would have some 12 us of weights left over and 17 copies more there, and took 0, up to 6. DVE's busy time there grew by 12.8 us, and by the one trace of e8 the products take 2.5 us more than in the kernel before for the same matmuls (355.1 for 352.6). So the 5.7 us are the price of the 48 and of this, less the 2 us of gap.

**Exponentials and sums, 0: held within the error.** e3 gives 2.2 us with an interval from 0 to 4.5, in the old order. A price of the hold of `xp`, put at nothing because other matmuls stand at the group's border, is not shown. In the new order DVE's eps waits 7.0 us for the last pv, as foreseen, and PE has no wait for the scaling that shows.

**Transposes, 0: held, by luck in the duration.** The issue was mis-sized (3.37 for 1.6 us) and the landing too (5.3 for 4.4), yet e1 shows 2 us for it, within the error. The slower rival, that PE would wait for 18-block transposes, did see the waits: they grew from 11.7 to 19.6 us, past the 12 that the prediction named as its sign, all of it in the first 150 us. But they were not what made the kernel slower: e1 and e12 take the 18-block transposes away, e1 has 9.3 us of these waits, and the loss stays.

**POOL and DVE.** The rival that POOL holds DVE up is not borne out as a cause: from 200 to 560 us DVE's low parts of hr took 0.791 us with POOL busy for 164 us, 0.792 with 155 [rows 9], and in the start, where the rival placed it, DVE waits for the scan anyway. The prediction read the 0.1 us of rows 9 as much less than a full block at each meeting. The mean hides what it is made of; the row of the changed kernel, and the same 30 instructions of the kernel before with the shortest, the median and the longest:

```profile
L1654 DVE TENSOR_TENSOR hr<-r,hr 128x512 f16<-128x512 f32 x9 | 7.1, 791 | 0.1
...
L1603 DVE TENSOR_TENSOR hr<-r,hr x30: 676/691/1655, 201.2 to 523.5; 128x512 f16<-128x512 f32 x30
```

At least half of them are not held up at all (0.691 us, for 0.688 while POOL was silent), and the longest took 0.96 us more than the median; a low part of hr on POOL takes 1.16 us in the median. That is what the rule that the prediction named from the Trainium skill (SBUF — State Buffer, section SBUF: two separate sides) would give, by which one of the two has the port pair for a whole instruction.

**The seam, +2: close in the number.** 131.3 us for 131.6, though DVE, which was to have 3.3 us more, was busy for 1.7 less there (114.35 for 116.04). That DVE's chain is the bound fits e13, where 48 matmuls less shorten the seam by 1 us only, and not e9, where 48 more lengthen it by 5.9: PE's work there has its price too.

**PE's waits, -2: wrong.** PE's idle time from the first norm to the last pv is 24.8 us for 19.7. What the low parts that POOL took over brought is not shown by any run alone.

**The chances.** Slower had 0.15, for a mechanism that was not it. The rival *off the path* (0.13), by which the 48 matmuls and the start's gain come back as waits, had more of what happened, but ended at no gain, 1053, since it gave the move no price at its new place. Last pv ended at 575.0 us where 557 was forecast, the first product began at 706.3 where 692 was. The prediction should have asked of each stretch what happens if PE's work there shrinks, instead of taking the busiest engine for the bound.

What stays open: of the 9 or 10 us, some 6 lie in the products. The other 3 or 4, which the ratio's interval leaves between nothing and 6, lie ahead of the last pv, where the changed kernel should have been up to 2.8 us earlier and is not. e12 says that they are not the ones column or the size of the transposes, e17 that the start's choice of engines, undone, does not give them back. Whether they are the rest of the order or the pairing of units (`hl` and `et` with two buffers of two units, both `pv` behind the second) was not tested, and which of the moved instructions it is was not found. Nor was the price of the 48 taken back in the changed kernel itself: e8 and e14 move them, and neither is faster.
